# Another hand-out of the same operations: a gated recurrence with a long convolution, one table of sequence replaced by another

## The chip, the cores and the metric

The kernel runs on one core of one Trainium2 chip, as a single launch. TensorE (PE) multiplies matrices and writes into PSUM, eight banks of 2 KB per partition; VectorE (DVE), ScalarE (ACT) and GpSimd (POOL) do elementwise work, and of these three POOL is never given an operand in PSUM here; SyncE (SP) issues all the DMAs. Each engine works through its own instruction stream in order and meets the others at semaphores. The metric is device microseconds of one execution, lower is better. The profile comes from one such execution.

## The reference

```python
B, S, D = 4, 6272, 256
# first part: a gated recurrence along the sequence
f = lower_bound + (1 - lower_bound) * sigmoid(f_logit)
h[t] = f[t] * h[t-1] + (1 - f[t]) * x[t]
# second part, with h as its input
x1, x2, x3 = split(h @ w_proj)                     # 256 -> 3 * 256
c = irfft(rfft(x2, axis=seq) * rfft(filter_fft, axis=seq))
out = (x1 * c * x3) @ w_out
```

`filter_fft` is a filter in time, despite its name: it is transformed too. The convolution is circular over 6272 = 128 * 49 positions.

## The kernel before

**Tiling.** A batch is one sequence of 6272 positions by 256 channels. The recurrence (`hgrn`, L312) takes it in 13 chunks of 512 positions, both channel halves of a chunk one after the other. For a chunk, SP loads `f_logit` into FL and `x` into XT (L321, operation `load`), ring buffers of three chunks each. ACT takes the sigmoid in place (L324, `sig`), POOL multiplies (L326, `u`), PE transposes both into PSUM for one channel half (L338, `su`), ACT or DVE makes the gate from PSUM (L351 or L353, `f`), and DVE runs the scan along the chunk (L359, `scan`) into the f16 tile HA. HA holds the sequence of each channel half, and behind it the first 3072 positions a second time, so that a column with stride 49 can be read without a turn. That second copy is made chunk by chunk by the operation `wrap` (L367 to L371), on POOL (a copy, L293), on ACT (a copy, L281), or by SP as a DMA from SBUF to SBUF (L291). There are 12 in a batch, 48 in all.

**Spectrum.** The 6272-point transform is done as 49 by 128. `phase_p` (L696, operation `P`, PE L705) multiplies 49 strided columns of HA by a part of `w_proj`, in 13 groups; ACT or DVE evicts each group into X2 (`x2`). `phase_f1` (`F1`, L718) and the `F2` of a unit (L777) are the forward transform of one of 16 units of channels; ACT or DVE evicts `F1` into a ring of four (`A`). In `unit` (L761) the spectrum is multiplied by the filter's: either DVE does it straight from PSUM (L798), or ACT or DVE copies it out (`prod`, L801) and POOL multiplies (L807, `pm`). The filter's spectrum of a unit lies in DRAM (tensors H) and is loaded by SP into Hu, a ring of three (L755, operation `H`). PE transforms back (`I2`, L817) and ACT or DVE evicts (`Th`, L822). Batches go through the units in alternate directions, so that the units still in Hu need no load: 55 loads in all.

**Gates and output.** `gate` (L374) makes x1 and x3 (operation `x13`, PE L387, two matmuls with 490 columns each), evicted by ACT or DVE (`xs`), and their product zt by POOL (L417, `z`) or by DVE straight from PSUM (L408). `phase_o` (L838) ends the inverse transform (`I1`, L851), DVE multiplies by zt (`y`, L857), PE multiplies by `w_out` (`proj`, L869), ACT or DVE scales into osb (`o`, L875, a ring of three) and SP stores (L879).

**Preparation.** Before the first batch the kernel makes its twiddle tables, scales the weights (operation `W`, ACT, L465 to L475; the raw weights lie where the second copy in HA will be) and transforms the filter (`ff`, `fr`, `rot`, `f2`, `FF1`, `afs`, `FF2`, `hw`), whose spectrum SP writes to DRAM in 16 DMAs (`hst`, L673). 24 groups of four idle matmuls (`warm`, L591) may be put anywhere.

**What sets the order.** Nothing is decided while the kernel is built. The functions above only append 2430 operations to a list, each with the engines that may do it. The string ORDER (L123) then names them in the order of emission, three characters to an entry:

```python
word = a * 4096 + b * 64 + c
yield word // 64, self.ENGINES[word // 8 % 8], word % 8
```

The first field is the operation's number, the second its engine out of ACT, DVE, PE, POOL, SP and MUL (DVE multiplies straight from PSUM, and the operation that POOL would have done emits nothing), the third the PSUM bank or pair of banks. `emit` (L106) calls the operations in that order. So the string holds the sequence on each engine, who evicts, and which bank each PE operation writes. An operation must come behind those that it depends on; apart from that, only the order on each engine counts, and the tile framework places the semaphores.

Of the kernel before, what the change touches and what calls it, by code (L numbers as in the profile page):

```python
# [59 lines left out]
class Plan:  # L60
# [63 lines left out]
    "A0gA1AA5gA6AA+gBDgBIgBNgBSgAAYAOYABIACIAPIApQAdQAzYAqQAoQAkQAyQARIA2QA/YA4AA3AAQAAVYAXYBXgAhSAlSBhgBAQBJYBCAAUIA"  # L124
    "WIAfSBBIA7SBEAAvUBcgBFUBOYBGEBHEAiWBKWBTYBLGBrgBMGBPUBREBYYAnWASABmgA9CA8KBwgBZWBiIBUQBdYBbOBVIBQEBjSBsYBlCBaGAT"
    "IBeUBgEBfEBnIBtWEFgAYYBuGBkCBWIBoUBxIAZYAaYBqEByQBzAB0AAxSD5gBpMB3SB4KD7AB5QB6IB7YBvOB+UD6gCASCBKB8QB/EB9AD8YCJU"
    "ADgAEYCKMCHSCDQCICCEICCYEHACQUCLYD9SERgETAEGgEBWD+KD/KEIYCREECGEDOCOQCPACMUCNEESgEUYCTQAFgCUAEJSEKKELKCXUCSYCYEE"
    "NQEdgB1YB2YEegEOAEVUAHAEfAEPIEgYEWMEXMEZWCeSCfCEpgEYYCZQCgSEaGEbOCaACcQCdICbYEqgCnUChCCiYE1gE2gEhSElWFBgCoMErAEs"
    "YAKAEiCFCgEjKEkYEmGEnOCpQCqACwUCrYAIACjQCxME3AE4YCkAEtSAJAEuKEvKExWFLgCuUGHgEyGEzOCvECyYCsQFMgFDAFEYE5UE6ME7ME9S"
    "CtAE+CFVgE/KEwYC5WE8YC6GCzQC0AC+WFNAFFUFIQFWgFfgFggFGMC2gC/GFJIDASC3WFOYDBCFHMC4GC7YDCYFXAFYYDHSC8WFKIFPUFQMFSQF"  # L130
    "pgFqgFRMC9GDICDDWDJSFTAFUIFZUFaMDEGDKCDLYFbMDOWFhAFiYFcQFzgF0gDPGFdAFeIDQSDRCDSYDZWDMUDTSFjQDNMCGgFrAFsYAGgDaGDU"
    "CFkIFlICmgDeWDfGDXUDYEDbYF1AF2YALADgSDhKFmWF9gF+gFnOFoODcUDdEFtQFuAFvIDpSCFgFwUDnWDqCDjSFxEFyMAMAE0YDiYEEYEcYEoY"
    "DoGDrYF/AGAYF3QF4IDkCFAYDuWDvOANAMegF5IDwUDxEC1gF6SF7CF8KEAYDsWEMYJbUJcVJeNMqgDyYJgQJhRGBSDtGClgJdECVgEQYJfYJiAG"
    "CKDzWJjBJkYGDKDWgGEUD3QGIgJlSJmTGFMGGMD0GD2gGtgJnKJorGJUGKED4ADVgGPWGQOGbSGcCGdUGeMGLQGMAGRSGSKGVUGWMMgAGXQGYIGZ"
    "SGaCDFgGTWGUOCWgMsAGNUGOMGhQGiIDGgGfSGgCJqWJrXD1gJvUJxMJwQJyoJzYJsGJtHJuYGjSGkCJ0RGpUGqEJ1QJ2BJ3IJ4YGuSGwqGxYGlW"
    "GmGJ5QGnUGoEJ7IJ6RDmgG/gJ+SJ/QKACGyqGzYDlgKDWKEXKBAJ8pKFGGrSKCYG2gG3UGsKGvYG7EKGvHAQHEAHRSHSCG5sKIVJ9YG8YKKFG6YG"
    "0WHCoKJRHDYG4YHBYHFYHXSHJUHYKG1GKLBHTWHUGG9QG+AHKYHVSHWCHGWHHGKNQKORMrgMtYJpYHIgHNsHOYHLsHMYKPAKHYKQBM2gM4AHZSHa"
    "KHcUKMYHdYHlWHnGHbgMfgKRYHesHfYHgsHhYHPSHmYHQCHkgHoYHtgKSQKTRKVJKXUKUAKZMHpuHqYH/VIAFHiSHjCIDQHuUIEAHvYIBWICGHrS"
    "HsCMhYHysHzYH3QH4YIFWIGGH2gKWYHwsHxYH0UH1EIKSH5oH6YH7oH8YIJgIHWIIOIMCINYILYIOqKYQKaoKbYITUISgIPYIVEIcRIeBH9WH+GI"
    "UYIXsIbgKcUKdTKeEKfrM3gItQIuAIQWIRGIWYKhUKiVKkFIdYIfYIkgKjMI3gMiQMjAIgpIhYKlYMkIIlWIpGIYYMmUMnEMoMNDgIZSIqYImYIa"  # L140
    "CM5YKmXKoHIiQIjAInuIoYIxSIyCMuUMvMMwMIvQIwAIzWI0GKnSKrTKtDI4QKpqNCgJAgI6oI7YI1UI2MI8AI9YJJgI5YMyWNOgMzGM0OJBSJDC"
    "NPgKqYNEANFYKsRKupJSgKwQKyAIrUJEYIsEKxSJFqJGYM6WM7GKzqM+QNagNbgM8OM/ANAIKgYI+UJLYI/EJCYK1TK2SK3DK0YK4qK5YNQANGUN"
    "RYNKWNmgNngNHEK6TNIMK8DNLGJTQJXAJVANMOJHSJUYJWYJICJKUNcAK7RJMsJNYK/QK9pK+YLBAJOsJPYNSSNTCLAWNUKLCGNdYLDYKvYLEULG"
    "ENWQNwgNxgNXALFXLJWLHvJQUNYINoANpYJRELKSLOTLPXLQDLRvNBgLSYNeUNiQN7gN6gLLGNfELMqJYYNgMNjANyANzYLTTLUWLYSLaCNkILVD"
    "LWuLXYLZXLbvLcYNqUNrENsMLIYLNYNtSOEgOFgNVANuCNvKJZQNhYJaAR7WR9GMpgR8XLdQLeIR+HN0ULiSLjKN8AN9YN1EN2MN3WOOgOPgN4GN"
    "5ONNYNZALfQLgALhgLkSLnULoMLlCN+QLmgN/AOAISAWSBXSCGNlYLsSLtKSDHOGAOHYOBUOYgOZgOCEODMLxWOQAORYLpQLyOLqALrgLuSLvCLw"
    "gL2UL3MOIQOJAOKIOLWOMGONOOigOjgLzSL0COSUL7QL8IOaAObYM9YNJYL1gOVSU+gOWCOXKMlAOTEOUMMxAL4WL5GL6gU/gL9QL+AL/gOkAOlY"
    "MASMBKMFWMGOOcUOdEOeMOfQVLgVKgOgAOhIMCSMDCMEgMHWM1YOmUOnEOpSOqCOoMOrKVWgMKQMLIMPUMQMMIGMJgO6SO7KO8WO9GPCQPDAO4UO"
    "5EO+SO/KPEQVAAVXgPFAVBYO0WO1GOuUOvEOyQOzIOwSOxKVMAVNYOsUOtMVYAO2QO3IPAWPBGMMSMNCMUUMVMPKQPLIVZYPGWPHGMRSMOgMSCMZ"
    "UMaMR/YSEYPQWPUuPVYPIQPJAPMUPNEMTgPSuPTYSFSSHKSGTSIDSJYMWQPOUPPMPZYPRYMXAPYWPogPauPbYPcuPdYPpSPrCPgUPkESKQSMAPWR"  # L150
    "PhYPlYPisPjYPXBPzVP0FP7gSLQSPXSRHSNoPeRPqYPtqPuYPsYSQUSUQSWIPfBPxWPyGSVVSXtSYYSSESTYP3SP4KP1QP2APmWP8UPnGQAsQBYP"
    "vQP5SP6KQGYP9YPwAP+sP/YQFWQHGQEgQIYQJuQKYSZVQNgSbFQfQQgAQXSQOVSaUQSFSeQSgAScsSdYQbKMYgQWgQCWQPYQTYQDGQQtQRYSfRSj"
    "QShpSiYSkTSlAQpgSmDQhWQiGQLUQYYQcYSnYQZqQaYQMEQjQQkAQUWQVGSOYQqUQygQusQvYSoSSqCQlQQmAQssQtYSpTQ7gQdWQeGSrrSsYStS"
    "SvCQnQQoIQrYQ0YQzUREgQ3EQ4YQ1sQ2YRFWRJGRHGRNSROKQwQQ9YQxAQ8UQ+ERAsRBYQ/YRXgVCWVDGRPQRQAVEOVGSVjgVigRggQ5URGYRIYR"
    "KYVHCVIKQ6ERpgVOQRCWVPAVQIRDGRRURSESuSSyTS0DSwqSxYRYWSzQRauRbYS1oS2YS3RS5BRcuRdYS4SRTUS8TS+LS6CS7YS9QVSRVvgVugRU"
    "ERVURWMRZYRygRLWRiYS/ATAYVTBVUJTBQRMGVkAVlYRhURjsRkYRlsRmYVaWVbGTDAReSRrYVcORfCTCRTGUTIETHQRqSRuqRvYTEBTFYVeUV7g"
    "V6gVmWTJATKYVFgVfEVgMRsCRtYVnGTLQTNATMRTQSTRTTOpTPYVoOVqUWHgWGgVwATSCTTrTUYVrEVsMRnQR0YVxYVJgRoATVSTWWTaXTXCTcHT"
    "bQTYuTZYRzSR1qR2YR3qR4YTdATeYV8ARwURxEVyQV2WWRgWQgVzAV0IV3GV4OTfSTgUTkTTiETlVTpUThCTqQTmDTntToYV9YTjYTrMWIAV+SV/"
    "CWCWWagTuRR5UTwBTvRWAKTzSTsoTtYTxpTyYWJYWDGWEOT0TT4QV1YR6EWbgT1CT2DT3YMbUT5RMcET6AT9SWKUWNWWSAWTYMdgT7pT8YWBAWkg"
    "WOGUCQWLEV5YWcAWdYWlgT+KT/SUACUBgUDIUEQUFAVdYWMMUHUWPOWUSWmAUIMUMWUGgWVCUNOWXQWWKWugWYAWZIWvgUJUUKEUOWUPGURSUSKW"  # L160
    "eUWhQWFYVVYWfEWgMULgVpAWiAW4gW5gabWUQgacXaeHWnYadGUTSUUCUVgUWUWwAWxYUbWWjIVhYUXMWoQWpAagSahTaiCajDUYUUZEUcOUgWWq"
    "IUhOWrSWyQXDgXCgWsCUdUWtKW1WWzAW0IW6AW7YW2GW3OUeEUagUiSUjCUlQUqUUmIUrMXEAXFYUfgdfgW8WW9GW+OW/SXACXBKdqgUnQUsUUoA"
    "UpgdegXGWXHGXJQd3gUkgXIOU0SVtYVRYXKAXLIU1KUtEUvWXiQXjAdrgUwOd2gXaUXbEXSSXTKXeQXfAXcUXdEXWSXXKdgAdsAXkQXlAdhYXOWX"
    "POUugdtYXYUXZEXMSXNKXgQXhAXUUXVMXQSXRCUxQUyAUzgU5UU6MafYXoSakYXmWXnOXpCXqUXrMXsQXtAalSanCamTaorU2WU3GU4gXuQXvIX5"
    "YXwUXyEX0sX1YXzYYIgdiSdjCX4QapYX8oX9YYTWYUGXxYX6oYbgaqUarVdkKasEavRatFaxBYAWYEGYCOauYdmUeCgdnEdoMX2QYBYX7YX3AYFY"
    "awXdlgayvYDYYkga0Sa2Ca1TX+QYKYa3ra4YYRUYSMazYd4Ad5YduWdySX/AeOga5QdvGdwOdzCd0KYVUa7AYWEa6Ra+Qa8BYJWYNuYOYYLuYMYb"
    "AAYXUYYEYGSYHCa/QbDRbBobCYa9Yd6UbFBYZSYaKYdYd7Ed8MYtgYcWYeGYfYYguYhYYPQYmYYQAYuSbEWYyCeDgYwCbGGYlQZBUZCEYnoYoYY2"
    "gbHYd+Seagd/CYpoYqYYiWYvYYjGeAKYxYZJgbIQbKAePgYzYbJUdpYbNVbLsbPFYrWY4YYsOZSgY/QeEAY3SY5qeFYY7qY8YZbgZFUZAAebgZGE"
# [779 lines left out]
```

## Time and profile before

| | |
|---|---|
| runs | 463.81, 460.79, 463.21 us, median 463.21 |
| profiled execution, first to last instruction | 460.2 us |
| busy: PE, DVE, ACT, POOL | 439.7, 412.1, 402.7, 310.2 us |
| DMA | 121.40 MB, 74.0% of 16 engines on the one queue that SP feeds |
| preparation and first recurrence, up to the first `P` | 0 to 75.5 us |
| batch 1, 2, 3, 4 by their first `P` | 75.5, 172.7, 273.0, 371.4 us |
| last group of `I1` to the end: first at | 432.8 us |

The profile gives no time of the profiled execution beyond its span of 460.2 us; the runs lie 0.6 to 3.6 us above it, and what lies around the span is somewhere in that. "Busy" joins overlapping instructions of an engine. A matmul's end is modelled, so that a busy PE need not be a PE at its peak. The recurrence of a batch is computed while the spectrum of the batch before is still under way, so the four batches overlap on all engines.

### The profile page before, as it was taken

How to read it: one execution, taken by the hardware profiler on the slowest of the kernel's cores; microseconds unless marked ns; L12 is line 12 of the kernel's file. 1: busy time of each engine (PE TensorE's matmuls, PEld its weight loads, DVE VectorE, ACT ScalarE, POOL GpSimd, SP SyncE). 2: the span in 40 equal slices, each digit the busy share in tenths (PEclk: the TensorE clock that was granted, in tenths of full speed). 3: DMA queues.
4: the chain of work that ended last, by engine and by line, in shares of the span. 5: the costliest groups of instructions: out<-in, count | busy, mean ns of one | idle time of the engine just before them, and what ended most of it. 6: DMA issues, size and time to landing. Idle time of an engine off the chain costs nothing.

```text
span 460.2 us, 14622 instructions
## 1 busy us (share of the span) xinstructions
PE 439.7 (96%) x6009; PEld 344.3 (75%) x6009; DVE 412.1 (90%) x471; ACT 402.7 (88%) x582; POOL 310.2 (67%) x293
## 2 busy tenths in 40 slices
PE   7799989999989999999999999999999999999997
PEld 5677778766756889778667889767768897777786
DVE  8689998899999996998999996999999987999872
ACT  6799988799999997899999988999998868989663
POOL 6889766188999643778898435789996603857400
PEclk9899999999999999999999999999999999999999
DMA  8967898986997997386887996579869830756176
GB/s 333 390 268 288 315 307 283 349 284 219 309 353 250 358 315 276 139 246 218 307 300 280 318 317 239 214 248 318 255 235 315 306 138 13 230 200 205 57 287 275
DMA packets 44242, 121.40 MB, mean 264 GB/s; under 512 B 4240, under 2 KB 6672, under 8 KB 44176
## 3 DMA queue, kind: packets, MB, share of 16 engines
q1 hardware_dynamic: 44176, 120.47, 74.0%
q8 instruction: 47, 0.77, 0.7%
q14 instruction: 19, 0.16, 0.1%
HBM read 87.69 MB, written 31.98 MB: 260 GB/s over the span
## 4 chain that ended last, share of the span: by engine, by line
PE 63%; DVE 12%; ACT 11%; DMA 5%; issue 5%; POOL 2%; SPq 0%; DVEq 0%; ACTq 0%; POOLq 0%
PE PS L387 14%; PE PS L817 8%; PE PS L869 7%; PE PS L338 7%; PE PS L705 6%; PE PS L777 6%; PE PS L718 5%; DVE HA L359 5%; PE PS L851 4%; DMA FL<-in_f_logit_dram 3%; DVE ys L857 2%; DVE X L286 2%; ACT FL L324 2%; PE PS L646 2%; ACT fTs L351 1%
## 5 line engine op out<-in xcount | busy, mean ns | idle before, releaser
L326 POOL TENSOR_TENSOR XT<-XT,FL 128x1024 f32<-128x1024 f32 (+1 forms) x52 | 116.9, 2251 | 50.3 <-ACT FL L324 41.9
L359 DVE TENSOR_TENSOR_SCAN HA<-fTs,HA,PS 128x512 f16<-128x512 f32 (+1 forms) x96 | 112.5, 1200 | 2.8 <-ACT fTs L351 1.7
L798 DVE TENSOR_TENSOR PP<-PS,Hu 98x1008 f16<-98x1008 f32 x87 | 101.3, 1197 | 3.4 <-ACT HA L281 1.4
L387 PE MATMUL PS<-HA,W 128*128 128x490 f16 (+1 forms) x416 | 100.4, 367 | 0.9 <-DVE X L286 0.4
L807 POOL TENSOR_TENSOR PP<-HA,Hu 98x1008 f16<-98x1008 f16 x41 | 86.2, 2107 | 1.7 <-PE PS L817 1.0
L281 ACT CAST HA<-PS 128x1024 f16<-128x1024 f32 (+1 forms) x94 | 77.0, 849 | 5.1 <-PE PS L718 3.4
L417 POOL TENSOR_TENSOR zt<-x1s,x3s 128x490 f16<-128x490 f32 (+1 forms) x43 | 52.3, 1222 | 41.8 <-ACT x3s L281 22.9
L857 DVE TENSOR_TENSOR ys<-PS,zt 128x1024 fp32r<-128x1024 f32 (+1 forms) x52 | 58.5, 1149 | 9.5 <-PE PS L851 5.0
L283 ACT ACTIVATE osb<-PS 128x1024 f32<-128x1024 f32 (+1 forms) x51 | 49.9, 992 | 13.9 <-PE PS L869 11.2
L351 ACT ACTIVATE fTs<-PS,nomc 128x512 f32<-128x512 f32 (+1 forms) x89 | 58.3, 679 | 3.7 <-PE PS L338 2.3
L387 PEld LDWEIGHTS <-W 128*128 128x128 f16 x416 | 35.4, 97 | 31.7 <-issue 5.4
L869 PE MATMUL PS<-Wo,ys 128*128 128x256 f32 x392 | 57.7, 292 | 1.3 <-DVE ys L857 1.1
L283 ACT ACTIVATE x1s<-PS 128x490 f32<-128x490 f32 (+1 forms) x92 | 53.5, 594 | 5.0 <-PE PS L387 3.0
L817 PEld LDWEIGHTS <-PP 98*128 98x128 f16 x1024 | 48.7, 98 | 10.6 <-issue 3.1
L324 ACT ACTIVATE FL<-FL 128x1024 f32<-128x1024 f32 (+1 forms) x52 | 53.0, 1026 | 2.2 <-DMA FL<-in_f_logit_dram 2.1
L869 PEld LDWEIGHTS PS<-Wo,ys 128*128 128x128 f32 x392 | 49.4, 188 | 5.8 <-DVE ys L857 2.2
L817 PE MATMUL PS<-VA,PP 98*128 98x98 f16 x512 | 52.2, 207 | 1.5 <-ACT x1s L283 0.8
L817 PE MATMUL PS<-VB,PP 98*128 98x98 f16 x512 | 51.9, 207 | 0.0
L281 ACT CAST Th<-PS 128x784 f16<-128x784 f32 x58 | 48.2, 830 | 2.6 <-PE PS L817 1.6
L338 PE MATMUL PS<-iden,FL 64*128 64x64 f32 x784 | 44.8, 230 | 1.6 <-DVE HA L359 0.9
L705 PE MATMUL PS<-W,HA 128*128 128x256 f16 x392 | 44.4, 273 | 1.0 <-ACT X L281 1.0
L705 PEld LDWEIGHTS <-HA 128*128 128x128 f16 x392 | 42.9, 142 | 1.9 <-issue 1.3
(113 smaller groups left out, 724.3 us busy)
## 6 DMA issues: line engine op xcount, KB each, us to landing
Hu<-H SPq DMA_DIRECT2D x55, 512.0 KB, 4.4
FL<-in_f_logit_dram SPq DMA_DIRECT2D x48, 512.0 KB, 5.4
XT<-in_x_dram SPq DMA_DIRECT2D x48, 512.0 KB, 5.5
out_dram<-osb SPq DMA_DIRECT2D x48, 512.0 KB, 4.3
X<-in_moe_filter_fft_dram SPq DMA_DIRECT2D x9, 512.0 KB, 7.1
H<-Hu SPq DMA_DIRECT2D x4, 512.0 KB, 6.2
Hu<-in_moe_filter_fft_dram SPq DMA_DIRECT2D x2, 512.0 KB, 9.8
H<-Hu SPq DMA_DIRECT2D x4, 256.0 KB, 6.5
```

The costliest lines, as they stand in the source:

```text
L281: nc.scalar.copy(dst, src)
L283: nc.scalar.activation(dst, src, AF.Copy, scale=scale)
L326: op("u", {"POOL": 0.1 + 0.553 * nb}, lambda e, xt=xt, ft=ft: nc.gpsimd.tensor_tensor(xt, xt, ft, op=AOP.mult), r=[("ft", k)], w=[("xt", k)])
L338: nc.tensor.transpose(bank(pb)[:, at[p] + j:at[p] + hn:nb], src[ps, j, cols], iden[ps, ps])
L359: nc.vector.tensor_tensor_scan(h, fT, bank(pb)[:, 512 - hn:512 + hn], init, op0=AOP.mult, op1=AOP.add),
L387: nc.tensor.matmul(PS[:, p, 0:n], W13[:, kh, js], HA[:, HB[kh] + t0:HB[kh] + t0 + n], start=(kh == 0), stop=(kh == 1))
L705: nc.tensor.matmul(pp[:, r - r0, :], column(HB[kh], q_of(r)), W2[:, kh, :], start=(kh == 0), stop=(kh == 1))
L798: nc.vector.tensor_tensor(pr, px.unsqueeze(1).broadcast_to([TB, 2, UE, 63]), hh, op=AOP.mult)
L807: nc.gpsimd.tensor_tensor(pr, spec[:, o, :, 1:64].unsqueeze(1).broadcast_to([TB, 2, UE, 63]), hh, op=AOP.mult)
L817: nc.tensor.matmul(PS[:, ib + o, pr * TB:(pr + 1) * TB], PP[:TB, k, o, n, 2 * pr:2 * pr + 2, :], v[:TB], start=(n == 0), stop=(n == 1))
L857: nc.vector.tensor_tensor(late["ys"][:, yk, :, 0:rn * 128], PS[:, cb:cb + 2, 0:rn * 128], late["zt"][:].rearrange("p k r m -> p k (r m)") ...
L869: nc.tensor.matmul(po[:, i, :], late["ys"][:, yk, kh, i * 128:(i + 1) * 128], Wo[:, kh, :], start=(kh == 0), stop=(kh == 1))
```

## The change

ORDER is replaced by another string. It has the same 2430 operations, and no line of the code is altered otherwise; it is two lines shorter, so that all line numbers behind it fall by two. Cut to the ends of both:

```diff
 ORDER = (
-    "A0gA1AA5gA6AA+gBDgBIgBNgBSgAAYAOYABIACIAPIApQAdQAzYAqQAoQAkQAyQARIA2QA/YA4AA3AAQAAVYAXYBXgAhSAlSBhgBAQBJYBCAAUIA"
...
-    "SAsSAcSAeQ"
+    "AAYA5gA0gAOYABIAlRBDgACIAfTA+gBNgAnXBIgAhQBXgAzYAPIBSgBhgA6ABcgA7WA1YAyVA8GAvVBrgA9GBEYAxUA2WBmgAdRA/IAQABFUA4OBwg"
...
+    "lmMlqWljClfglvQlrOlnUlkglsWloElwIl0SltGlpglxQl1Klugl5WlyAl2Tl6OlzgArSl3Dl7QAbVl4gAwUl8IAcXl9gAeQAsQAgUAtTAjQ"
 )
```

Decoded, the two differ in who does an operation as follows (all other kinds are alike, the 87 products and all scans on DVE among them):

| operation | before | after |
|---|---|---|
| `wrap` | POOL 34, ACT 8, SP 6 | POOL 20, ACT 2, SP 26 |
| `x2` | ACT 27, DVE 25 | ACT 32, DVE 20 |
| `xs` | ACT 131, DVE 16, MUL 61 | ACT 127, DVE 21, MUL 60 |
| `f` | ACT 89, DVE 15 | ACT 88, DVE 16 |
| `o` | ACT 51, DVE 1 | ACT 49, DVE 3 |
| `prod` | ACT 39, DVE 2, MUL 87 | ACT 38, DVE 3, MUL 87 |
| `f2`, `fr`, `afs`, `hw` (preparation) | ACT 60, DVE 21, POOL 7 | ACT 58, DVE 22, POOL 8 |

The sequence on PE is the same in large stretches and differs in detail: the groups of `P` within a batch come in another order, neighbours change places throughout, and the groups of idle matmuls stand partly elsewhere (behind the last `proj` eight of them, four before). On SP the 20 further copies stand among the loads and stores; in the first batch 15 of the 16 `hst` stand before the first `P`, 9 before. PSUM banks are dealt anew with the order.

More of the change, by code (lines that the diff above doesn't have):

```diff
@@ L129 @@
[L129 to L168, printed above, removed]
```

86 lines of the change are left out of this document (62 added, 24 removed).

## Prediction

> **What bounds the kernel now.** First the busy times and the chain of work that ended last, from the page:
>
> ```profile
> PE 439.7 (96%) x6009; PEld 344.3 (75%) x6009; DVE 412.1 (90%) x471; ACT 402.7 (88%) x582; POOL 310.2 (67%) x293
> ...
> DMA  8967898986997997386887996579869830756176
> ...
> PE 63%; DVE 12%; ACT 11%; DMA 5%; issue 5%; POOL 2%; SPq 0%; DVEq 0%; ACTq 0%; POOLq 0%
> ```
>
> PE is the bound, with DVE and ACT a few per cent behind, and the DMA row is at 8 or 9 tenths over most of the first third. The change leaves every matmul in place, so only PE's lost time can move. To size that, I took for each kind of PE operation the lower quartile of the time from its start to the next one's, apart for a next one that uses 64 rows of the array and one that uses 128 (`su` 548 and 603 ns, `F1` 447 and 542, `x13` 413 and 506, `I2` 695 and 790). Summed over the 762 operations that is 424.9 us; from the first matmul to the last the trace has 455.7. So some 31 us are lost to waits: about 14 before the first `P` at 75.5 us, 8 in the first batch, 5 and 3 in the next two. That is all there is to win. Next, busy time by stretches (us, then PE, PEld, DVE, ACT, POOL busy with their counts, granted clock, DMA share, GB/s):
>
> ```profile
> 15.00:24.00 9.00, 6.87 (x35) 5.09 (x34) 5.75 (x9) 7.08 (x14) 7.58 (x12) 0.81 1.02 387
> ...
> 75.50:172.70 97.20, 92.72 (x1368) 71.78 (x1366) 90.53 (x98) 88.32 (x128) 69.31 (x55) 1.00 0.88 303
> ...
> 371.40:432.80 61.40, 61.07 (x748) 46.77 (x748) 54.70 (x64) 50.86 (x75) 34.33 (x35) 1.00 0.42 141
> ```
>
> The reader is to see that the loss lies where DMA is busiest: share 0.88 in the first batch with 4.5 us of idle PE, 0.42 and almost none in the last. The granted clock is below 1 only at 15 to 24 us.
>
> **The change part by part.** I decoded both tables and counted.
>
> *PE itself.* Changes between 64 and 128 rows, about 0.096 us each by the pairs above: 238 before, 236 after. **-0.2 us.**
>
> *ACT, DVE, POOL.* With each operation at its mean by engine (`wrap` 0.620 on ACT and 0.612 on POOL, `x2` 1.065 on ACT and 1.225 on DVE, `xs` 0.592 and 0.677, `o` 0.99, `f` 0.68 on both), the sums of durations go from 453.3 to 448.3 on ACT, 438.7 to 438.4 on DVE, 323.8 to 317.8 on POOL. POOL's six are covered: it is idle a third of the span. ACT's five count only where PE waits for ACT. Such a place, on ACT's timeline:
>
> ```profile
> 163.64 0.68 ACT L351 ACTIVATE fTs<-PS,nomc 128x512 f32<-128x512 f32 x1
> 164.21 0.62 ACT L281 COPY HA<-HA 128x512 f16<-128x512 f16 x1
> 164.72 0.70 ACT L351 ACTIVATE fTs<-PS,nomc 128x512 f32<-128x512 f32 x1
> 165.30 0.63 ACT L281 COPY HA<-HA 128x512 f16<-128x512 f16 x1
> 165.81 1.95 ACT L283 ACTIVATE osb<-PS 128x1024 f32<-128x1024 f32 x2
> ```
>
> The two copies (starts 164.21 to 164.72, 165.30 to 165.81) hold up an osb eviction that the chain of waits contains from 165.93. Both leave ACT: 1.0 us. A third, at 354.4, stands just ahead of an osb eviction in the chain at 355.64: 0.5 us. The five `x2` that go to ACT lie in `P`, where a group takes PE 0.87 us and two engines evict: covered. Bounds: nothing, and all of ACT's 4.9. I take **-1.5.**
>
> *Copies as DMAs.* Twenty more copies are issued by SP. What one costs, from the DMA queue's issues and from the line of the copies:
>
> ```profile
> HA<-HA SPq DMA_DIRECT2D x6, 128.0 KB, 5.0
> ...
> DMA to landing us min/median/max: 4.4/5.0/5.9
> ```
>
> A POOL copy ends 0.6 us after its start, a DMA copy 5. Mostly it is wanted much later. In the first batch it is not: the raw weights lie where the copy goes, so the first chunk's copies wait for the last weight conversion, and the first `P` reads them. Before, POOL makes them:
>
> ```profile
> 70.03 0.67 ACT L475 CAST Wo<-HA 128x512 fp32r<-128x512 f32 x1
> ...
> 75.70 4.37 PE PS L705 x40
> ```
>
> From the conversion's end (70.70) to the first `P` (75.5) are 4.8 us, and the tables put 5.9 (before) and 5.4 us (after) of PE work between the two. After, SP issues behind that conversion one copy (0.47 us), a load of x (0.4), then a copy that the first group of `P` reads: 0.1 + 0.9 + landing. At 4.4 us it is late by 0.6. DMAs issued between 71 and 76 us landed after 5.3 to 7.3 us; at 7.3 it is late by 3.5. Behind the waiting `P` stands everything on PE. Bounds 0 (the table may leave more room than I count) and +3.5; I take **+2.0.**
>
> The Trainium skill, page "DMA: Bandwidth & Descriptors", section "Anatomy of one DMA — SWDGE (gpsimd) path", fits a DMA as about 2.0 us plus its bytes over 436 GB/s, which for 128 KB is an estimate of 2.3 us. By that the copy lands in time, this term is 0 and the sum below 2 us lower; the six copies of this trace, 4.4 to 5.9 us, disagree, and the fit is for the other issuing path.
>
> *The filter's spectrum.* In the first batch DVE waits 1.0 us for Hu, and the chain has "100.43 6.23 DMA Hu<-H": PE loses 1.9 us at 100 to 110 us against 1 elsewhere. After, 15 of 16 `hst` and the first three H loads are issued earlier, and fewer loads of the next batch stand between the H loads. Bounds 0 and -1.9; **-1.0.**
>
> *SP's queue.* SP issues in order, and whoever waits there holds up the rest:
>
> ```profile
> SPq L879 <- ACT osb L283: 109.4, 42, 16.9
> SPq L321 <- PE PS L338: 84.4, 37, 10.8
> ```
>
> Two places are new. In batch 2's recurrence a store that waits for its `o` stands ahead of the x load of chunk 12 of 13 (before, both loads stand ahead of it), and behind that load wait `u` and `su`: between nothing and 1.8 us, and I take the lower middle, **+0.7.** At the end of that recurrence the last copy of chunk 6 stands behind a load that waits for a buffer; it lands about 6.4 us after that `su`, at the moment when the third group of `P`, its first reader, starts: 0, at most +1.5.
>
> *DMA volume.* 20 x 128 KB is 2.6 MB on 121.4. DMA holds 5% of the chain, 23 us; 2.2% of that is **+0.5**, between 0 and +2 (the 128 KB at 264 GB/s are 0.5 us each, and four may hit a load that is waited for).
>
> *End.* Four idle groups follow the last `proj` now, eight after, at 0.44 us. Before, PE ends at 457.6 and the last store lands at about 458.9 (issued 456.3, landing 2.6); with eight PE ends at about 459.4. **+0.5**, between 0 and +1.8.
>
> *Preparation.* Its evictions, casts and idle matmuls are dealt anew; the trace can't show it. The first 75 us lose 14 us in either direction of luck; a fifth of that, 3 us, bounds it from both sides. **0.** A new half-clock stretch as at 15 to 24 us (0.19 of 9 us lost, 1.7) lies within.
>
> Sum: -0.2 - 1.5 + 2.0 - 1.0 + 0.7 + 0.5 + 0.5 = **+1.0 us**, on the profiled 460.2 a span of 461.2. The median run is 3.0 above that span; what differs is added to it: **464.2 us**.
>
> **The rivals.** *Slower: loads late behind SP's copies.* A chunk's buffer must come back through load, `sig`, `u` and the transposes: 5.4 + 1.03 + 2.25 us and some waits. The trace shows it from 41.1 (free) to 49.7 and from 55.1 to 65.2, 8.6 and 10.1 us, while PE has 7.3 to 12 us of other work per round. A copy ahead of a load costs 0.46 us of issue and 0.5 of transfer. About 18 of the 26 stand between loads of a running recurrence; if 8 meet a round that is already late, it is 8 x 0.96 = 7.7 us, less the -0.2 and the -1.5 of ACT kept: 463.2 + 7.7 - 1.7 = **469.2 us**. It decides once f_logit loads land after more than about 6.5 us; in the trace the four issued at 119.7 to 132.2 us took 6.4 to 7.1, those in the recurrences after them mostly 3.5 to 4.9. Against it: most copies stand behind the load that is waited for.
>
> *Faster: ACT's relief counts in full.* The copies land in slack, ACT's 4.9 us count, and the spectrum's 1.0: 463.2 - 0.2 - 4.9 - 1.0 = **457.1 us**. For it: in the second and third batch ACT is busy 92.6 of 100.3 and 91.5 of 98.4 us. Against it: DVE, unchanged, is as busy there (93.6 and 91.3), and ACT holds 11% of the chain.
>
> **How the numbers follow.** One per cent is about what a measurement of this kernel can tell from no change (the runs spread 0.65%), so the borders are 458.6 and 467.8. My forecast, a sum of terms of both signs that nearly cancel, gets 0.55; the slower rival, with late first copies or an unlucky preparation on top, 0.28; the faster one 0.17. Adding the open ends in squares gives 5 us down and 5 up around 464.2, 459 to 469 for the forecast alone; the range reaches towards both rivals, 457 to 471.
>
> **What would show it.** Right: the first `P` starts 1 to 3 us after 75.5, with a wait of the weight load of L703 for a DMA copy; in the first batch less waiting for Hu; ACT busy 398, POOL 304; from the first `P` to the end as long as before within 2 us. Wrong: a first `P` at 75 or sooner; sigmoids waiting for f_logit by over 5 us in all (2.1 now); a stretch at half clock beyond the present one; or batches shorter by 2 us each, which would mean that ACT was the bound.

## The result, and the profile after

The changed kernel takes **478.47 us** (median of four runs, 476.54 to 481.31) against 463.32 us (460.79 to 463.81) for the kernel before: a ratio of 1.035, with a 95% interval of 1.030 to 1.040. The prediction said 464.2 us, 457 to 471. The profiled execution has a span of 479.5 us, 19.3 more than before. Ratios here and below are of the fast runs of each kernel, those within 1.5% of its fastest.

The page of the changed kernel: busy times, DMA share in 40 slices, shares of the chain that ended last.

```profile
PE 447.0 (93%) x6009; PEld 348.4 (73%) x6009; DVE 412.6 (86%) x475; ACT 402.8 (84%) x571; POOL 305.2 (64%) x281
...
DMA  8959989947898999177877996269898830558276
...
PE 51%; DVE 13%; DMA 13%; ACT 10%; POOL 6%; issue 6%; DVEq 0%; SPq 0%; ACTq 0%; POOLq 0%
```

PE is busy 7.3 us longer than before, DVE and ACT as long and POOL 5.0 us less, so most of the 19.3 us are new idle time. In the chain DMA goes from 5% (23 us) to 13% (62 us) and PE from 63% to 51%: the path now runs through transfers. The waits of the computing engines for transfers, in the table of waits (what waits, for what; us in total, times, longest), first before and then after:

```profile
POOL XT L326 <- DMA XT<-in_x_dram: 2.4, 3, 1.5
ACT FL L324 <- DMA FL<-in_f_logit_dram: 2.1, 2, 1.2
ACT osb L283 <- DMA out_dram<-osb: 1.9, 2, 1.7
DVE PP L798 <- DMA Hu<-H: 1.0, 2, 0.7
```

```profile
POOL XT L324 <- DMA XT<-in_x_dram: 9.6, 5, 3.3
ACT FL L322 <- DMA FL<-in_f_logit_dram: 6.0, 6, 2.0
DVE PP L796 <- DMA Hu<-H: 4.5, 5, 1.9
ACT osb L281 <- DMA out_dram<-osb: 4.3, 4, 1.7
DVE osb L286 <- DMA out_dram<-osb: 3.7, 1, 3.7
```

Loads, spectrum loads and stores are all late now. By stretches, the middle two batches before, and then the four batches after (us, then busy times with counts, granted clock, DMA share, GB/s; a batch from its first `P` to the next one's, the last to its last group of `I1`):

```profile
172.70:273.00 100.30, 98.43 (x1443) 77.56 (x1442) 93.56 (x99) 92.60 (x135) 72.06 (x59) 1.00 0.76 268
273.00:371.40 98.40, 96.99 (x1426) 76.57 (x1425) 91.27 (x97) 91.50 (x135) 72.92 (x59) 1.00 0.75 261
```

```profile
78.60:182.60 104.00, 97.16 (x1367) 74.30 (x1367) 88.12 (x96) 88.17 (x126) 65.52 (x51) 0.97 0.85 290
182.60:287.50 104.90, 99.96 (x1443) 78.07 (x1441) 93.22 (x99) 92.82 (x134) 69.33 (x55) 1.00 0.77 260
287.50:390.20 102.70, 97.52 (x1428) 76.92 (x1425) 92.91 (x100) 91.24 (x131) 70.87 (x55) 1.00 0.72 252
390.20:451.70 61.50, 60.73 (x737) 45.62 (x736) 53.87 (x65) 50.16 (x71) 39.13 (x39) 1.00 0.45 149
```

The first batch before has 97.20 us, 92.72 of them with PE busy, as the prediction shows. The loss is spread: 3.1 us before the first `P` (78.6 for 75.5), 6.8, 4.6 and 4.3 in the first three batches, 0.5 in the last, which loads no next batch. In the first batch most of it is longer busy time of PE, 4.4 us of 6.8, in the only stretch whose granted clock is below 1 (0.97). In the second PE's busy time grows by 1.5 us of 4.6 only and in the third by 0.5 of 4.3; the rest is idle PE. With the prediction's lower-quartile base, PE's lost time, from one operation's start to the next one's, goes from about 31 to about 53 us: +3.4 in the preparation, and behind it about +6 ahead of transposes (`su`), +4 ahead of `x13`, +3 ahead of `F1`, +2.5 ahead of `P`, +1.3 ahead of `proj`.

One place in full, SP's part of the timeline and then PE's, POOL's and ACT's (start, duration, engine and line; in brackets the idle time just before and what ended it):

```profile
163.25 0.34 SPq L319 DMA_DIRECT2D FL<-in_f_logit_dram  x1
166.46 0.33 SPq L877 DMA_DIRECT2D out_dram<-osb  x1
166.88 0.39 SPq L319 DMA_DIRECT2D XT<-in_x_dram  x1
...
173.60 2.35 POOL L324 TENSOR_TENSOR XT<-XT,FL 128x1024 f32<-128x1024 f32 x1 [4.79 <-PE PS L849]
...
175.09 0.42 ACT L322 ACTIVATE FL<-FL 128x256 f32<-128x256 f32 x1 [2.05 <-DMA FL<-in_f_logit_dram]
...
176.01 0.46 PE L336 MATMUL PS<-iden,XT 64*128 64x64 f32 x8 [1.46 <-POOL XT L324]
```

These are chunk 12 of the second batch's recurrence. Its buffers are free at 163.4. SP issues the load of f_logit at once, but the load of x stands behind a store that waits for its `o`; it goes at 166.88 and lands 6.6 us later, at 173.45. POOL has idled 4.8 us when `u` starts right behind (the bracket names PE, which had nothing to do with it), and PE waits 1.5 us. Before, the same load was issued 0.25 us after its buffer was free. Over the 39 chunks of batches 2 to 4, loads of x issued more than 2 us after their buffer was free (the end of the last transpose that reads it) number 10 before and 22 after.

### The profile page after: what moved, and what is told of

It reads as the page before. It is cut to its first block, busy times and chain, and to the rows that moved or that the text cites. A ratio compares the mean times of both kernels' runs of the same rounds, so it can differ in the third digit from the quotient of the medians.

```text
span 479.5 us, 14653 instructions
## 1 busy us (share of the span) xinstructions
PE 447.0 (93%) x6009; PEld 348.4 (73%) x6009; DVE 412.6 (86%) x475; ACT 402.8 (84%) x571; POOL 305.2 (64%) x281
## 4 chain that ended last, share of the span: by engine, by line
PE 51%; DVE 13%; DMA 13%; ACT 10%; POOL 6%; issue 6%; DVEq 0%; SPq 0%; ACTq 0%; POOLq 0%
PE PS L385 10%; PE PS L703 9%; PE PS L867 6%; PE PS L336 6%; PE PS L815 5%; DMA out_dram<-osb 5%; PE PS L716 5%; DVE HA L357 4%; PE PS L775 4%; DVE PP L796 4%; DMA Hu<-H 3%; POOL XT L324 3%; DMA FL<-in_f_logit_dram 3%; PE PS L849 2%; POOL PP L805 2%
## 5 line engine op out<-in xcount | busy, mean ns | idle before, releaser
L385 PE MATMUL PS<-HA,W 128*128 128x490 f16 (+1 forms) x416 | 102.5, 367 | 2.6 <-ACT osb L281 0.7
L415 POOL TENSOR_TENSOR zt<-x1s,x3s 128x490 f16<-128x490 f32 (+1 forms) x44 | 53.7, 1227 | 43.2 <-DVE ys L855 19.3
L867 PE MATMUL PS<-Wo,ys 128*128 128x256 f32 x392 | 59.2, 298 | 0.5 <-ACT osb L281 0.2
L281 ACT ACTIVATE x1s<-PS 128x490 f32<-128x490 f32 (+1 forms) x90 | 51.8, 584 | 6.4 <-PE PS L385 3.7
L867 PEld LDWEIGHTS PS<-Wo,ys 128*128 128x128 f32 x392 | 51.0, 193 | 5.1 <-DVE ys L855 0.7
L703 PE MATMUL PS<-W,HA 128*128 128x256 f16 x392 | 46.0, 279 | 3.1 <-POOL zt L415 1.2
L336 PEld LDWEIGHTS PS<-iden,FL 64*128 64x128 f32 x784 | 33.7, 138 | 20.3 <-DVE HA L357 6.4
```

The costliest lines, as they stand in the source:

```text
L281: nc.scalar.activation(dst, src, AF.Copy, scale=scale)
L336: nc.tensor.transpose(bank(pb)[:, at[p] + j:at[p] + hn:nb], src[ps, j, cols], iden[ps, ps])
L385: nc.tensor.matmul(PS[:, p, 0:n], W13[:, kh, js], HA[:, HB[kh] + t0:HB[kh] + t0 + n], start=(kh == 0), stop=(kh == 1))
L703: nc.tensor.matmul(pp[:, r - r0, :], column(HB[kh], q_of(r)), W2[:, kh, :], start=(kh == 0), stop=(kh == 1))
L867: nc.tensor.matmul(po[:, i, :], late["ys"][:, yk, kh, i * 128:(i + 1) * 128], Wo[:, kh, :], start=(kh == 0), stop=(kh == 1))
```

## The experiments

**The theories.** A: the 20 further copies on SP cost the time. B: it is SP's order among loads, stores and spectrum loads, in which waiting transfers hold up others. C: it is the order on PE, the banks, the evictions and the preparation, whatever the transfers do. D, formed after the first four runs: the changed table asks for data with less slack than the transfers take. Ratios are to the kernel before; the changed kernel has 1.035.

### Copies and SP's order, changed one at a time

```diff
 # ORDER of the changed kernel, decoded: the engine of 27 copies, at their places
-wrap half 1 chunk 1 of batch 1   SP
-wrap half 2 chunk 2 of batch 1   SP
+wrap half 1 chunk 1 of batch 1   POOL
+wrap half 2 chunk 2 of batch 1   POOL
...
```

> The changed table, with nothing altered but the engine of the `wrap` copies: each is made by the engine that makes it in the table before (POOL 34, ACT 8, SP 6 in place of POOL 20, ACT 2, SP 26), at its place in the changed sequence. Theory A (the 20 further copies on SP cost the time: late data, SP's issue time, DMA traffic): 463 to 467 us, with most of the 15 us back. Theory B (SP's order among loads, stores and spectrum loads costs it): the loads still land as late, 474 to 478. Theory C (the order on PE, the banks, the preparation): 476 to 480, since ACT and POOL get work back.

Measured: 475.1 us, ratio 1.028 (1.023 to 1.033). Only some 3 us come back, give or take 3: by theory A most should have. The reverse edit on the kernel before:

```diff
 # ORDER of the kernel before, decoded: the same 27 copies, at their places
-wrap half 1 chunk 1 of batch 1   POOL
-wrap half 2 chunk 2 of batch 1   POOL
+wrap half 1 chunk 1 of batch 1   SP
+wrap half 2 chunk 2 of batch 1   SP
...
```

> The table before, with nothing altered but the engine of the `wrap` copies: each is made by the engine that makes it in the changed table (26 by SP in place of 6), at its place in the sequence before. Theory A: 473 to 479 us, with sigmoids that wait 5 us or more for f_logit (2.1 before) and `u` that waits for x. Theories B and C: 461 to 466, as before.

Measured: 476.6 us, ratio 1.031 (1.027 to 1.036). The number is A's, but the way isn't. `u` and the sigmoids hardly wait for loads; PE waits inside `P` for the copies (PE and weight loads in the table of waits):

```profile
PE PS L703 <- DMA HA<-HA: 9.6, 2, 6.4
...
PEld L703 <- DMA HA<-HA: 6.5, 1, 6.5
```

Behind the longer of these waits PE's granted clock is halved for 10.2 us (length, then the columns as above):

```profile
176.00:186.24 10.24, 4.94 (x24) 3.78 (x25) 2.00 (x2) 1.01 (x1) 0.00 (x0) 0.50 0.73 284
```

PE is busy for 4.9 us of it, so up to 2.5 us of the 14 are work at half speed. In the changed kernel the same wait is 1.2 us in all, because its table issues the copies at other places. So what a copy on SP costs depends on its place, and the changed table has placed most of them harmlessly: A explains about a fifth there. Next SP's whole sequence, and then its order without the copies:

```diff
 # the kernel before, SP's sequence from the changed table; PE, ACT, DVE, POOL as before but for the copies
 load f chunk 12 of batch 2
-load x chunk 12 of batch 2
 store batch 1
+load x chunk 12 of batch 2
 store batch 1
 load f chunk 13 of batch 2
+wrap half 2 chunk 2 of batch 2
 load x chunk 13 of batch 2
+load f chunk 1 of batch 3
 store batch 1
-load f chunk 1 of batch 3
 store batch 1
...
```

> The table before on PE, ACT, DVE and POOL, with their banks and evictions, but SP's whole sequence (loads, copies, stores, spectrum transfers) and the engines of the copies from the changed table. If the cost lies in what SP does (A and B together): 473 to 480 us. If it lies in the order on PE and in the preparation (C): 461 to 466. A rise here beyond that of the kernel with only the copies on SP is theory B's.

Measured: 484.4 us, ratio 1.051 (1.045 to 1.058). What SP does is enough to produce a loss larger than the whole change's.

```diff
 # as the last one, but the copies stay on the engines of the kernel before
 load f chunk 12 of batch 2
-load x chunk 12 of batch 2
 store batch 1
+load x chunk 12 of batch 2
 store batch 1
 load f chunk 13 of batch 2
 load x chunk 13 of batch 2
...
```

> The table before on all engines, copies too (POOL 34, ACT 8, SP 6), but SP's other transfers (loads, spectrum loads and transfers to H, stores) in the order of the changed table. Theory B (that order by itself makes data late): 468 to 475 us. If only the copies on SP make it harmful: 461 to 465. With the copies as well it took 484.4, and the copies alone 476.6.

Measured: 477.3 us, ratio 1.031 (1.026 to 1.037). The order alone does it, with 121.4 MB as before. Its table of waits shows the loads:

```profile
POOL XT L324 <- DMA XT<-in_x_dram: 22.4, 8, 9.1
ACT FL L322 <- DMA FL<-in_f_logit_dram: 8.4, 7, 4.7
```

A sum of POOL's waits says little by itself: with the copies back it was 35.0 us for x, and that kernel is faster than the changed one, where it is 9.6. But the time is plain. So B holds in the table before: nothing but the order in which SP issues the same transfers costs some 14 us. Then the cure, on the changed table:

```diff
 # the changed table, SP's transfers in order of readiness; all other engines as changed
 load f chunk 12 of batch 2
-store batch 1
 load x chunk 12 of batch 2
+wrap half 2 chunk 2 of batch 2
+store batch 1
 store batch 1
 load f chunk 13 of batch 2
-wrap half 2 chunk 2 of batch 2
 load x chunk 13 of batch 2
...
```

> The changed table with SP's sequence alone put in another order: each transfer (loads, copies, spectrum loads, stores) at the place where what it waits for is there, so that a spectrum load which waits for its buffer no longer stands ahead of loads and copies that could go. All transfers and all other engines as in the changed table. Theory B (waiting transfers at the head of SP's queue hold up others): 470 to 475 us. If the queue's order does not matter: 477 to 480.

Measured: 474.7 us, ratio 1.024 (1.018 to 1.029). Loads of x issued over 2 us late fall from 22 to 4, and PE's lost time ahead of transposes by nearly 5 us, but ahead of `P` it rises by some 3. By the ratios some 5 us come back, 11 remain. So late issue of these loads is not most of the loss on this side; they land later here, after a median of 6.6 us for x where the changed kernel has 6.0. (The order was worked out from the times in the changed kernel's trace, so it is near readiness and not exactly that.) Both cures at once:

```diff
 # the changed table: copies on the engines of the table before, and SP in order of readiness
 load f chunk 12 of batch 2
-store batch 1
 load x chunk 12 of batch 2
 store batch 1
+store batch 1
 load f chunk 13 of batch 2
-wrap half 2 chunk 2 of batch 2
 load x chunk 13 of batch 2
...
```

> The changed table with the copies made by the engines of the table before, and SP's transfers in order of readiness: the two edits that gave 3 and 4 us alone. If the two are separate parts of the cost: 470 to 472 us. If both relieve the same waits: 474 to 475. If the late loads behind them vanish with both: 463 to 467.

Measured: 474.2 us, ratio 1.024 (1.019 to 1.028): no more than one of them. The parts add up neither on this side (3 and 5 give 5, each give or take 3) nor, by the ratios, on the other (14 and 14 give 24).

### The preparation, and stages

```diff
 # ORDER: entries up to the first P of the first batch from the table before, the others from the changed one
-prefix: changed table
+prefix: table before
 rest: changed table
```

> Hybrid: every engine goes through the table before up to its first `P` (75.5 us), and what is left comes in the order, on the engines and in the banks of the changed table. By the stage marks of the two traces 3 of the 15 us arise before the first `P`: 474 to 477 us if each stage costs by itself, whatever its cause. 463 to 467 if the later stages only carry on a lag (of loads or of DMA work) that the preparation leaves behind.

Measured: 477.6 us as the median of four runs between 472.8 and 481.0; the ratio, 1.026 (1.021 to 1.031), is of the two shorter ones. By the ratio about 4 us come back, by the median of all four hardly any, so this run doesn't settle what the preparation costs. In its profiled execution, one of the longer ones, the first `P` still started at 78.7 us, with the clock at half for 6.8 us from 20.9 us on, where the profile of the kernel before has 3.4. With the other two cures on top:

```diff
 # ORDER: prefix from the table before; in the rest, copies as before and SP in order of readiness
-prefix: changed table
+prefix: table before
-rest: changed table
+rest: changed table on PE, ACT, DVE and POOL
...
```

> Three parts of the change undone at once: the table before up to its first `P`, the copies on the engines of the table before, and SP's other transfers behind that in order of readiness; PE, ACT, DVE and POOL keep the changed order from the first `P` on. Copies and readiness together gave 474.2, the preparation alone 477.6. If the preparation's 3 us (17.7 us of lost PE time against 14.4) add to the others: 469 to 472 us. If the whole lies in these three: 463 to 466. If they relieve the same waits: 473 to 476.

Measured: 474.8 us, ratio 1.024 (1.015 to 1.033). Three undone parts give back no more than one. Some 2% are left for how the order on PE, ACT, DVE and POOL from the first `P` on meets the transfers, unless a still better order on SP would take them away.

```diff
 # ORDER: entries up to the first P of the third batch from the table before, the others from the changed one
-prefix: changed table
+prefix: table before
 rest: changed table
```

> Hybrid: every engine goes through the table before up to the first `P` of the third batch (273.0 us), and what is left comes in the order, engines and banks of the changed table. By the stage marks the changed table lost 4.3 us in its third batch and 0.5 behind it: 466 to 469 us if each stage loses by itself. 463 to 465 if the later stages only carried on a lag from the earlier ones; 472 or more if the seam itself costs.

Measured: 473.2 us, ratio 1.021 (1.013 to 1.029), more than the 4.8 us that the later stages had lost. The seam costs something itself (the profile has two windows at half clock, 6.8 us together, from 280 us), so this run doesn't settle whether the stages lose independently.

### The transfers made small

The edits are shortened to what changes. The loads of the first three chunks and the first three spectrum loads stay whole.

```diff
 # the changed kernel; the same edit on the kernel before
+    cut = nb if count["x"] <= NX else 1
-    dst, src[b, t0:t0 + n, :].rearrange("(p j) d -> p j d", p=128)
+    dst[:, 0:cut], src[b, t0:t0 + n, :].rearrange("(p j) d -> p j d", p=128)[:, 0:cut]
...
-    Hu[:, h].rearrange("p a e k -> p a (e k)"), turned(H[u // 2][u % 2])
+    Hu[:, h].rearrange("p a e k -> p a (e k)")[:, :, 0:256], turned(H[u // 2][u % 2][:, 0:256])
...
-    out[b].rearrange("(a r) d -> a r d", r=Q)[:, r0:r0 + rn, :], late["osb"][k][:, 0:rn, :]
+    out[b].rearrange("(a r) d -> a r d", r=Q)[:, r0:r0 + 1, :], late["osb"][k][:, 0:1, :]
```

> The changed table with short transfers: from the fourth chunk on a load brings a quarter of f_logit and x (one of four rows of each partition), from the fourth spectrum load on H brings a quarter of a unit, and a store sends a quarter of osb; the rest of the chunk, of the spectrum and of out is left out. Every instruction, wait and copy stays. Theory D (the changed table asks for data with less slack, and loses the 15 us because loads, spectrum loads and stores take 4.4 to 6.2 us to land): 457 to 465 us. Theory C (the order on PE, the banks and the evicting engines cost it, whatever the transfers do): 473 to 478.

> The table before with the same short transfers (a quarter of each load from the fourth chunk on, of each spectrum load from the fourth on, and of each store; the rest is left out). Theory D: the table before hides its transfers, so it gains little, 456 to 462 us, and stands within 5 us of the changed table with short transfers. Theory C: it stays 13 to 17 us ahead of that.

Measured: the changed table 459.9 us, ratio 0.994 (0.990 to 0.997); the table before 456.9 us, ratio 0.988 (0.983 to 0.993). With 47 to 49 MB in place of 121 to 124, the changed table gains 18 us and the one before 5, and 3 of the 15 us between them are left. So theory C, with its loss whatever the transfers do, holds for 3 us at most, and the other 12 hang on the transfers, as D says. Part of the 3 goes with the clock: the three executions of the changed table with a mean granted clock of 1.0 took 457.4 to 457.9 us, the three of the table before 456.5 to 456.9. Part of the 12 may be the clock too: with whole transfers, three of the changed kernel's four runs have 0.989, but the fourth, with 0.996, still took 476.5 us. Which transfers?

```diff
 # the changed kernel: only the load's two lines of the edit above
+    cut = nb if count["x"] <= NX else 1
-    dst, src[b, t0:t0 + n, :].rearrange("(p j) d -> p j d", p=128)
+    dst[:, 0:cut], src[b, t0:t0 + n, :].rearrange("(p j) d -> p j d", p=128)[:, 0:cut]
```

> The changed table with short loads of f_logit and x alone (a quarter from the fourth chunk on; the rest of each chunk is left out), spectrum loads and stores in full. Theory D, with the loads as the late transfers: 465 to 471 us. If the spectrum loads or the stores are the late ones, or under theory C: 475 to 479.

Measured: 462.3 us, ratio 1.002 (0.998 to 1.006). Cutting the loads alone brings the changed table to the time before, below the range expected. But also:

```diff
 # the changed kernel: only the spectrum load's and the store's lines of the edit above
-    Hu[:, h].rearrange("p a e k -> p a (e k)"), turned(H[u // 2][u % 2])
+    Hu[:, h].rearrange("p a e k -> p a (e k)")[:, :, 0:256], turned(H[u // 2][u % 2][:, 0:256])
...
-    out[b].rearrange("(a r) d -> a r d", r=Q)[:, r0:r0 + rn, :], late["osb"][k][:, 0:rn, :]
+    out[b].rearrange("(a r) d -> a r d", r=Q)[:, r0:r0 + 1, :], late["osb"][k][:, 0:1, :]
```

> The changed table with loads in full, but spectrum loads and stores cut to a quarter (from the fourth spectrum load on; the rest of the spectrum and of out is left out), which takes away as many bytes (about 40 MB) as the short loads did. Theory D1: 470 to 476 us, since only what is late of H and osb, and what the loads gain from emptier queues, comes back. Theory D2: 460 to 466, as with the short loads.

Measured: 464.2 us, ratio 1.003 (0.999 to 1.007). Taking 39 MB away from other transfers cures it as well. (The table before was not run with either cut; with all transfers short it gained 5 us, so up to that much may be a gain that any table has.) So it is not the load as such. The test of that gives the bytes back without anybody waiting for them:

```diff
 # the changed kernel with short loads
+    if src is x and cut < n // 128:
+        aside = dram.tile([128, 6 * D], F32, name=f"aside{b}_{t0}")
+        nc.sync.dma_start(aside[:], x[b, 0:768, :].rearrange("(p j) d -> p (j d)", p=128))
```

> The changed table with the short loads of f_logit and x (a quarter from the fourth chunk on, the rest of each chunk left out), but behind each pair of them SP issues one more transfer, from DRAM to DRAM, of the 768 KB that the pair no longer brings; nothing waits for it. Theory D1 (the loads' own lateness costs the time): 462 to 468 us, near the 462.3 of the short loads alone. Theory D2 (their 39 MB of traffic make the copies, stores and spectrum loads late): 473 to 480.

Measured: 484.6 us, ratio 1.048 (1.041 to 1.056), even more than the changed kernel and above the range expected; SP has 45 more transfers to issue, which write DRAM as well as read it, and which of this adds the 6 us isn't shown. The loads bring a quarter of the bytes still. From the pages' lists of DMA issues (count, KB each, median us to landing), the short loads without that traffic, then with it:

```profile
FL<-in_f_logit_dram SPq DMA_DIRECT2D x49, 128.0 KB, 2.9
...
HA<-HA SPq DMA_DIRECT2D x26, 128.0 KB, 3.4
```

```profile
aside<-in_x_dram SPq DMA_DIRECT2D x45, 768.0 KB, 6.7
...
FL<-in_f_logit_dram SPq DMA_DIRECT2D x49, 128.0 KB, 4.8
...
HA<-HA SPq DMA_DIRECT2D x26, 128.0 KB, 5.6
```

A load of 128 KB takes 4.8 us where the queues are full and 2.9 where they aren't; a copy, unchanged in both, 5.6 and 3.4. The landing time belongs to the traffic more than to the transfer.

```diff
 # the changed kernel
+    cut = nb if count["x"] <= NX else min(nb, 2)
-    dst, src[b, t0:t0 + n, :].rearrange("(p j) d -> p j d", p=128)
+    dst[:, 0:cut], src[b, t0:t0 + n, :].rearrange("(p j) d -> p j d", p=128)[:, 0:cut]
```

> The changed table with loads of f_logit and x that bring half a chunk from the fourth on (two of four rows of each partition; the rest is left out): about 24 MB less, 100 of 124 MB. Quarter loads (88.7 MB) gave 462.3. If the loss falls evenly with the traffic: 467 to 470. If there is a point from which the queues hide everything, and it lies near the present traffic: 462 to 465.

Measured: 466.9 us, ratio 1.010 (1.004 to 1.017). For the changed table the time is 462.3, 466.9 and 478.5 us at 89, 100 and 124 MB: 0.4 and 0.5 us for each MB, an even fall rather than an edge.

### Full queues, or too little slack?

Counting each transfer from its issue to its landing, a transfer meets on average 2.6 others in flight before and 3.2 after; before, the median landing takes 3.9 us with one other in flight at the issue (51 transfers), 5.4 with three (54) and 6.6 with five (17). That looked like a cause by itself: a table that bunches its transfers. So both tables got more traffic:

```diff
 # the kernel before; the same edit on the changed kernel
     nc.sync.dma_start(dst, src[b, t0:t0 + n, :].rearrange("(p j) d -> p j d", p=128))
+    if src is x and more and n == CH:
+        aside = dram.tile([128, 2 * D], F32, name=f"aside{b}_{t0}")
+        nc.sync.dma_start(aside[:], x[b, 0:256, :].rearrange("(p j) d -> p (j d)", p=128))
```

> The table before, and behind each pair of full loads from the fourth chunk on SP issues one more transfer of 256 KB from DRAM to DRAM, for which nothing waits: 45 of them, 11.5 MB, a tenth more traffic. If the table before stands at the edge of what the DMA queues can hide, and the changed table is past it (E): 470 to 480 us, as if the order had been changed. If the table before has slack against traffic that the changed one lacks (S): 463 to 466.

> The changed table with the same 45 transfers of 256 KB that nothing waits for. E and S alike: worse by more than the 11.5 MB take on a queue that is busy 74% of the time, 484 to 492 us. Under S the table before loses 10 us less by them; under E both lose about the same.

Measured: the table before 466.4 us, ratio 1.012 (1.007 to 1.016); the changed one 486.4 us, ratio 1.052 (1.046 to 1.059). In the table before the transfers now meet 3.6 others in flight, more than in the changed kernel, and its loads of f_logit and x land after a median of 5.8 and 6.4 us over all 52, where the changed kernel has 5.6 and 6.0. Yet it stays 12 us ahead of it, and these are its waits for loads:

```profile
ACT FL L326 <- DMA FL<-in_f_logit_dram: 5.8, 9, 1.1
...
POOL XT L328 <- DMA XT<-in_x_dram: 2.6, 3, 1.6
```

`u` waits for x by 2.6 us in all, hardly more than the 2.4 of before. Bunching falls as the cause by itself. The table before loses 4 to 5 us by the added bytes, where slack had said 1 to 4 and the edge 8 or more, and the changed table loses 8: nearer to slack, but not free of the traffic.

Slack can be read from the traces, as the time from a landing to the first use:

| | before | changed | before, more traffic |
|---|---|---|---|
| x to `u`, median | 3.1 us | 1.6 us | 2.0 us |
| of 52, used within 0.3 us | 3 | 11 | 8 |
| f_logit to its sigmoid, median | 2.0 us | 1.4 us | 1.3 us |
| of 52, used within 0.3 us | 3 | 12 | 15 |

The changed table does have less slack at its loads. But under more traffic the table before has hardly more, and it still stays 12 us ahead. What differs is how much of the lateness gets through to PE: ahead of transposes PE loses about 1 us more than before there, and 6 in the changed kernel. So slack at the loads isn't the whole of D; why the order before keeps PE at work beside late loads isn't shown.

Last, the one exchange that the prediction had priced, in the table before:

```diff
 # the table before, SP's sequence
 load f chunk 12 of batch 2
-load x chunk 12 of batch 2
 store batch 1
+load x chunk 12 of batch 2
 store batch 1
```

> The table before with a single exchange on SP, the one that the prediction priced at +0.7 us: in the second batch's recurrence the store stands ahead of the load of x of chunk 12 of 13, as in the changed table (there the load was issued 3.4 us after its buffer was free, in the table before 0.25). By the prediction's step: 0 to +1.8 us. If such single places carry the loss: +2 to +4 us, 464.5 to 467, with `u` of that chunk waiting for x. If the order before has slack enough for one such place: no difference, 462 to 463.5.

Measured: 462.3 us, ratio 0.999 (0.995 to 1.003). The load is held up here too:

```profile
153.17 0.34 SPq L319 DMA_DIRECT2D FL<-in_f_logit_dram  x1
156.38 0.33 SPq L877 DMA_DIRECT2D out_dram<-osb  x1
156.80 0.39 SPq L319 DMA_DIRECT2D XT<-in_x_dram  x1
```

Its buffer was free at 153.35, so it is issued 3.45 us late and lands at 163.2. POOL's waits for x rise from 2.4 to 7.5 us, and the kernel takes no longer: PE's lost time is 31.6 us, 31.3 before. One late load is absorbed. By the interval one exchange costs between -2 and +1 us, SP's whole changed order some 14.

**What stays open.** Shown: some 12 of the 15 us hang on the transfers under the traffic of this kernel, SP's order alone can make such a loss in the table before, and neither copies, nor SP's order, nor the preparation holds it alone on the changed side. Not separated: how the remaining 2% divide between the order on PE, the evicting engines and the banks, and how much the halved clock adds to the waits. A fourth buffer for loads, which would give slack directly, wasn't tried. No kernel that computes the whole output was faster than the one before.

## Why the prediction was wrong

The likeliest way, terms of both signs that nearly cancel, failed. Term by term:

- **PE's row changes, -0.2.** Nothing speaks against it; it is too small to be seen. But it prices the row changes alone, and for what else the new order on PE and the evicting engines does behind the first `P` the sum has no term.
- **ACT's relief, -1.5.** ACT's busy time didn't fall to 398: it is 402.8 us, 402.7 before. The sum of its instructions' durations did fall, from 457.1 to 447.8 us in the traces, but they overlap less, and nothing shows that any of it reached the end.
- **The first `P` behind an SP copy, +2.0.** The mechanism was right, and so was the place. The copy is issued behind the last weight conversion, the chain waits for its landing, and `P` runs on from there:

```profile
71.64 0.61 ACT L473 CAST Wo<-HA 128x512 fp32r<-128x512 f32 x1
...
72.27 1.28 SPq L289 DMA_DIRECT2D HA<-HA  x1
...
74.25 0.57 SPq L289 DMA_DIRECT2D HA<-HA  x1
...
80.16 12.23 PE L703 MATMUL PS<-W,HA 128*128 128x256 f16 x95 [1.24 <-DMA HA<-HA]
```

  The copy lands after 5.8 us, within the 4.4 to 7.3 that the prediction gave, and behind a single matmul at 78.62 `P` runs from 80.16, against 75.70 before. It was issued 2.0 us after the conversion's end, not 1.0, since the copy ahead of it took 1.28 us to issue. PE waits 1.2 us for it, and another 1.2 before the single matmul; that wait ends just behind the landing of the copy ahead, at 78.38, and an operation on POOL that the profile names ends at about the same time. So the term, 2.0 between 0 and 3.5, fits with 1.2 to 2.5. The rest of the 4.5 us is older. The chain before, and the chain after:

```profile
66.61 0.71 PE PS L338 x16
```

```profile
68.33 0.71 PE PS L336 x16
...
74.25 5.78 DMA HA<-HA
```

  These transposes already start 1.7 us later. From them to `P` are 9.1 us before, 11.8 after, 10.5 with the copies back on POOL and 9.7 with the preparation from the table before; the first `P` runs from 79.1 and 78.8 us in those two, since their transposes start at 68.6 and 69.1. What makes the transposes late isn't settled, and with the preparation's order from before they come late too.
- **The filter's spectrum earlier, -1.0.** The gain didn't come. The half-megabyte `hst` land after 8.0 us (6.2 before), and the first load of H goes at 86.1 us where it had gone at 78.0: later, not earlier. In the first batch DVE's waits for Hu are 0.7 us, 1.0 before, but POOL has a new one of 0.9. The rise of DVE's sum from 1.0 to 4.5 us lies in the later batches, mostly in the second (3.0).
- **SP's queue, +0.7.** This is the step that failed. It named two new places by hand and priced each by itself. The first behaved as described and within its bound: 3.4 us of late issue, 1.5 us of waiting PE, and alone in the table before it costs nothing that can be seen (0.999, so 0.7 isn't refuted). But SP's order as a whole costs some 14 us (1.031) there. Of the 243 transfers that aren't copies, 188 have another neighbour ahead or behind; the step treated the order as two exceptions in an otherwise unchanged queue. The sum also has nothing for how the new order on the other engines meets the transfers: with the copies and SP's order both put right, 11 of the 15 us are still there (1.024).
- **DMA volume, +0.5.** It scaled DMA's 23 us in the chain by the bytes; they became 62. Pricing bytes by the mean rate missed how landing times grow with what is in flight: loads of x from 5.5 to 6.2 us, stores from 4.3 to 5.2, half-megabyte `hst` from 6.2 to 8.0. Near the present volume a MB costs the changed table 0.5 us, so the 2.6 MB alone would be 1.3; the run with the copies back gives 3 for bytes, issues and places together.
- **End, +0.5.** Right for the stage by luck: 89.3 us from the last batch's first `P` to the end, 88.8 before. Behind the last `proj` itself it takes 6.0 us, 4.3 before, near the bound of +1.8, and in another way than described: the last eviction waits for a store to land, and five of the eight idle groups wait for that eviction. The chain after:

```profile
470.84 4.86 DMA out_dram<-osb
...
476.30 2.34 PE PS L589 x20
```

- **Preparation, 0 within 3.** By the first `P` +3.1, with the copy's term in it; by the transposes above, which come ahead of these copies, +1.7: within its bounds.

**The slower rival** was the right family with the wrong culprit and less than half the price. Loads are late, but its deciding point, f_logit landing after more than 6.5 us, wasn't reached by the median (5.6): part of them are late because they are issued late. It put that on the copies, 8 of them at 0.96 us, and gave 469.2; taking the copies back gives 3 us, and the order of stores, spectrum loads and loads among themselves makes more. Whether most copies stand behind the load that is waited for is beside the point. **The faster rival** needed ACT's relief to count; ACT's busy time had none.

Of what was to show it, some came: the first `P` 3.1 us later with a wait for a copy, POOL busy 305 us, a little less waiting of DVE for Hu in the first batch. What mattered came out against the forecast: from the first `P` to the end it takes 16.2 us more, not within 2; ACT's busy time is what it was; the sigmoids wait 6.0 us for f_logit, over the 5 set as the mark of a wrong prediction; and there are new stretches at half clock.

The Trainium skill, page "DMA: Bandwidth & Descriptors", section "Anatomy of one DMA — SWDGE (gpsimd) path", gives 2.3 us for a copy of 128 KB as an estimate, for another issuing path. The copies took these times here (issue in ns, and landing):

```profile
L289 SPq DMA_DIRECT2D HA<-HA x26: 471/496/1588, 52.4 to 361.9; - x26
...
DMA to landing us min/median/max: 3.4/5.7/7.8
```

With loads, spectrum loads and stores cut to a quarter the median copy, still of 128 KB, takes 2.3 us: the estimate is met there, and not under this kernel's traffic.

## What to carry to other kernels

Where an in-order queue issues all transfers, a table of sequence can't be judged by the few places that look new: here one late load was absorbed and the whole order was not. Count over all transfers when each is issued, when it lands and when its data are wanted, and look at what PE has to do meanwhile; late issue alone explained only a part. Landing times under load are a property of the traffic: take them from transfers in the same stretch, and take a quarter of the bytes away in both kernels to learn how much of a difference is waiting for data at all. Parts of such a change needn't add: here the copies were worth 3 us undone and 14 done alone.

## What the runs showed of the hardware

- A transfer of 128 KB landed after 2.3 us with the traffic at 49 MB in 459 us, 3.4 at 89 MB and 5.7 at 124 MB (copies of HA, medians).
- Issuing a transfer took SP a median of 0.38 us in the changed kernel, 0.50 for a copy, and up to 1.6; with none or one issued in the 4 us before the median was 0.36, with four 0.54. Every transfer behind it waits for that too.
- PE's clock was halved for one more 3.4 us window in the first `P` and one in the second batch's recurrence, each after PE had waited and each, like the one from 20 us on before, in a stretch whose DMA share is about 1:

```profile
80.00:86.00 6.00, 5.84 (x38) 5.09 (x39) 1.23 (x1) 2.58 (x3) 0.43 (x1) 0.72 1.04 400
176.00:182.00 6.00, 5.59 (x64) 5.08 (x65) 3.26 (x5) 3.75 (x7) 1.28 (x2) 0.72 1.01 375
```

  Each costs up to 1.7 us, together 3.4 of the 19.3 us by which the spans differ. In the 3.4 us ahead of the two windows PE was busy for 1.4 and 1.9. In the profile with short loads the extra windows are gone. More traffic alone doesn't bring them: the table before with 45 transfers more shows none. That the waits do, so that late data are paid for twice, fits all of this, but no run separates it.
